# A fourth buffer for u, squares and gates left in PSUM, and another order for every engine

## The chip, the cores and the metric

The kernel runs on one core of a Trainium2 chip. The metric is device time in microseconds of one execution. The core has TensorE (PE), VectorE (DVE), ScalarE (ACT), GpSimd (POOL) and SyncE (SP), each with its own in-order list of instructions; DMA queues move data between device memory and the on-chip SBUF; matmul results land in PSUM, which has eight banks.

## The reference

Three layers follow one another, over 4 batches of 768 tokens with 384 channels.

```python
# attention: 8 heads of 48 channels, a state per head that decays by channel
f = 1.0 / (1.0 + np.exp(-f_logit))
for t in range(S):
    state = f[:, :, t, :, None] * state + np.einsum('bhd,bhe->bhde', k[:, :, t], v[:, :, t])
    y[:, :, t] = np.einsum('bhd,bhde->bhe', q[:, :, t], state)

# first MLP (x is y with the heads side by side)
h = gelu_tanh(x @ w_in)                       # 384 -> 1024
u, v = h[..., :512], h[..., 512:]
v_n = (v - mean(v)) / np.sqrt(var(v) + 1e-06) * g_ln
v_s = np.einsum('ts,bsd->btd', w_sg, v_n) + b_sg[None, :, None]
x = x + (u * v_s) @ w_out

# second MLP
h = np.maximum(x @ w_in2, 0.0)                # 384 -> 1024
conv = sum over 3 neighbouring tokens of conv_w[k] * h
out = (h * sigmoid(conv)) @ w_out2
```

## The kernel before, in words

**Units.** The attention is cut into 24 units, one per batch and chunk of 128 tokens (`Attention.plan`, L310). Four pairs of heads stand side by side on 112 partitions. One unit is a chain. SP loads the logits (`load_f`, L362), k and q (`load_kq`), and v. ScalarE takes the sigmoid (`decays`, L377). VectorE scans the decays forwards (`forth`, L383), takes the reciprocals of the ends (`turn`, L388), scans backwards (`back`, L396) and multiplies k and q by the products (`scale`, L408). TensorE transposes k (`turn_k`, L415: T in the text), ScalarE copies it (`keep_k`, L420), TensorE makes the state's update (`update`, L466: up). VectorE makes two states: the middle one (`middle`, L476, or a copy at L474 for a batch's first unit) and the one behind the unit (`behind`, L482 and L483), which the next unit needs. TensorE then multiplies q by the states (`states`, L496: st) and k by q (`scores`, L429: sc); VectorE masks the scores (`seen`, L436), and TensorE multiplies them by v (`values`, L512: va). ScalarE copies the output in two halves (`outs`, L525) and SP stores it.

**First MLP.** A batch's items stand in the string `SEQ`: L loads half of x (three units' outputs), v makes one 128-token part of v with its gelu and normalization (`vpart`: V), u one part of u with its gelu (`upart`: U), s one product with w_sg, which is scaled and gated (`sg`: S), and o one output (`out1`). Every fp32 operand is split into a high part (a ScalarE cast, L659) and a low part (a VectorE subtraction, L664), and each product is made of three matmuls (`mm3`, L653). The weights come as 64-bit numbers: one ScalarE pass (L578) and six VectorE instructions (`narrow_steps`, L579 to L591) narrow a piece.

**In a V**, ScalarE takes the gelu from the PSUM bank into SBUF with a sum (L908), GpSimd makes the mean (L911), ScalarE squares into a bf16 tile `junk` that nobody reads, for the sum alone (L914), GpSimd makes the root (L920, L921) and an offset (L924), ScalarE normalizes (L927). **In an S**, VectorE scales the bank into an SBUF tile `gt` (L996) and multiplies by u (L1002).

**What sets the order.** Every piece of work is a task, with the engine, an estimate of its time, the tasks that it follows, and the buffers that it takes and uses. `Order.run` goes through the tasks like a clock: of those of an engine that could begin soonest it writes the one with the lowest rank from the table `DUE`; then the engine's list is fixed. A task that takes a buffer of a ring (`RINGS`) waits there until the one that held it is free of its users. V, U and S take one of three PSUM banks (`M=3`); five more (`MA`) are opened when the attention is done. The second MLP follows (`second`).

Of the kernel before, what the change touches and what calls it, by code (L numbers as in the profile page):

```python
# [11 lines left out]
BF16 = mybir.dt.bfloat16  # L12
# [11 lines left out]
P = 128  # L24
# [43 lines left out]
class Order:  # L68
# [41 lines left out]
    def start(self, t):  # L110
        at = self.free[t.eng]
        for a in t.after:
            e = a.end + (HOP if a.eng != t.eng or a.kb else 0.0)
            if e > at:
                at = e
        for n in t.take:
            e, _ = self.soonest(n)
            if e is None:
                return None
            if e > at:  # L120
                at = e
# [32 lines left out]
    def write(self, at, t):  # L154
# [32 lines left out]
        -548.7, -477.3, -161.3, -153.1, 189.4, 212.0, 364.9, 430.2, 591.1, 816.0, 698.7, 736.9,  # L187
        909.1, 1157.3, 1295.0, 1375.7, 1376.1, 1739.4, 1653.8, 1761.4, 3751.4, 2011.8, 2225.9, 3838.8,
    ],
    "unit front": [  # L190
        1385.3, 859.0, 1060.5, -250.2, 1511.2, 1703.3, 1812.9, 2025.9, 2365.2, 229.0, 604.9, 1897.4,
        3788.3, 1201.6, 3779.5, 3805.2, 631.9, 182.0, 1139.5, 3820.9, 1390.5, 1533.0, 2401.4, 499.2,
    ],
    "unit": [
        638.3, 737.0, -203.3, 127.0, 277.0, 425.3, 534.2, 705.8, 1362.3, -576.0, 881.6, 507.0,
        -609.2, -479.0, 1608.3, 211.3, -646.7, -160.9, 210.1, 700.3, 716.4, 533.3, 2213.5, 868.7,
    ],
    "unit out": [
        2412.2, 992.5, 1073.9, 2426.6, 757.2, -615.8, 2198.6, -642.0, 890.0, 1138.3, 1022.7, 1151.8,
        197.2, 624.4, 886.7, 466.3, 991.0, 1980.1, 2189.4, 1392.3, 2317.7, 1151.9, 471.3, 1300.2,  # L200
    ],
    "weight load": [
# [3 lines left out]
    ],  # L206
    "weight": [
# [21 lines left out]
    ],  # L229
    "item then": [  # L230
# [20 lines left out]
POOL_RATE = 0.0021  # L251

# [9 lines left out]
class Attention:  # L262
# [12 lines left out]
    def __init__(self, nc, tc, ctx, cst, f, kq, v, xd):  # L275
# [21 lines left out]
        self.stored, self.scaled = {}, []  # L297

# [7 lines left out]
    def plan(self, S, u):  # L306
# [9 lines left out]
        lf = add("SP", 0.38, self.load_f, kind="unit load", take=["ft"], kb=224)  # L316
        lk = add("SP", 0.38, self.load_kq, kind="unit load", take=["kin"], kb=448)
        lv = add("SP", 0.38, self.load_v, kind="unit load", take=["vt"], kb=192)
        ft, kin, vt = lf.hold["ft"], lk.hold["kin"], lv.hold["vt"]
        sig = add("ACT", 0.63, self.decays, lf, kind="unit front", uses=[ft], table="sigmoid")  # L320
        fw = add("DVE", 1.23, self.forth, sig, kind="unit front", uses=[ft], take=["pr"])
# [4 lines left out]
        kq = add("DVE", 1.23, self.scale, bw, lk, kind="unit front", uses=[pr, kin])  # L326
        self.scaled.append(kq)
        tr = add("PE", 0.6, self.turn_k, kq, uses=[kin], take=["T"])
        k2 = add("ACT", 0.53, self.keep_k, tr, uses=[tr.hold["T"]], take=["k2"])
        up = add("PE", 0.8, self.update, k2, lv, self.scored, uses=[k2.hold["k2"], vt], take=["A"])  # L330
        a1 = up.hold["A"]
        mid = add("DVE", 0.36, self.middle, up, before, uses=[a1], take=["mid"])
# [11 lines left out]
        s7 = self.scored = add("PE", 0.92, self.scores, s5, kq, uses=[kin], take=["A"])  # L344
# [7 lines left out]
        s6 = add("PE", 0.78, self.values, cm, s5, lv, uses=[a2, cm.hold["sm"], vt])  # L352
# [117 lines left out]
    def middle(self, u, st):  # L470

        mid = st["mid"] = self.wp.tile([R, NP, D], F32, tag="mid", bufs=2, name="mid")
        if u % NCH == 0:
            self.nc.vector.tensor_copy(mid, st["pu"][0:R, 0])  # L474
        else:
            self.nc.vector.tensor_tensor(mid, st["pu"][0:R, 0], self.st[u - 1]["new"], op=ALU.add)  # L476

    def behind(self, u, st):
# [4 lines left out]
        self.nc.vector.tensor_tensor(new, new, pe, op=ALU.mult)  # L483
# [122 lines left out]
class Mlp:  # L606


    RINGS = dict(M=3, early=2, stg=2, x0=1, x1=1, vg=2, u=3, xr=2, gt=1)
# [85 lines left out]
    def low(self, n, terms, lo, after, rank, uses):  # L695
# [10 lines left out]
        m = box["m"] = S.add("PE", 0.25 + n * 0.0023, mm, after=after, rank=rank, take=["bank"], uses=uses)  # L706
# [61 lines left out]
    def prep(self, w_in, w_sgt, w_out, g_ln, conv_w, b_sg, pace):  # L768
# [5 lines left out]
        self.junk = self.mp.tile([P, FH], BF16, name="junk")  # L774
# [45 lines left out]
        t3, hold, c = self.narrow(conv_w.bitcast(I32).rearrange("p (n two) -> p n two", two=2), "early", 12, [pace[2]])  # L820
        t3 = S.add("DVE", 0.17, lambda: nc.vector.tensor_copy(self.cols[:, KH:], c()), after=[t3], rank=due("weight", 12), uses=[hold])
        self.t_w["g"] = [t, t2, t3]
# [20 lines left out]
    def load_x(self, b, hf, after, item):  # L843
# [11 lines left out]
        ld = S.add("SP", 0.38, load, after=after, rank=due("item", item), take=["stg"], kb=590)  # L855
# [34 lines left out]
    def vpart(self, b, n, item):  # L890
# [38 lines left out]
        m = box["m"] = S.add("PE", 2.09, mm, after=self.t_x[b, hf] + self.t_w["v"], rank=rank, take=["bank", "vg"], uses=[x])  # L929
# [4 lines left out]
        t = S.add("ACT", 0.93, square, after=[t], rank=then, uses=[vg])  # L934
# [15 lines left out]
    def upart(self, b, hf, db, item):  # L950
# [12 lines left out]
        def gelu():  # L963
            u = self.u[b, hf, db] = self.mp.tile([P, HALF], F32, tag="u", bufs=3, name="u")
# [4 lines left out]
            1.57,  # L969
# [558 lines left out]
```

## Time and profile before

| | us |
|---|---|
| median of 3 runs | 598.56 (597.53 to 599.43) |
| the profiled execution, its own time | 596.89 |
| its span in the trace | 595.2 |
| TensorE busy | 547.0 (92% of the span) |
| VectorE busy | 440.7 (74%) |
| ScalarE busy | 361.8 (61%) |
| GpSimd busy | 68.1 (11%) |
| mean granted TensorE clock | 0.988 |

The profiled execution is 1.67 us under the median of the runs. Its span leaves out 1.7 us around it. In tables of stretches, the busy time of each engine stands beside the number of its instructions; in a timeline, the bracket at a row's end is the idle time just before it and what ended it.

### The profile page before, as it was taken

The page shows a single profiled execution, that of the slowest core. Times are in us where ns is not written, and L with a number is a line of the kernel's source. Part 1 is how long each engine was busy: PE and PEld are TensorE (multiplying, and loading weights), DVE is VectorE, ACT ScalarE, POOL GpSimd, SP SyncE. Part 2 cuts the span into 40 slices and gives each one's busy share as a digit, 9 for nine tenths or more (in the row PEclk, how much of TensorE's full clock was granted, in tenths as well). Part 3 has the DMA queues.
Part 4 walks back from the last instruction along what each step waited for, and adds up shares of the span by engine and source line. Part 5 has one row for each costly group of instructions (what it writes and reads, how often), then busy time and mean ns, then how long its engine had stood idle before and what let it go on. Part 6 is the DMA issues. An engine that isn't in the chain of part 4 may idle for free.

```text
span 595.2 us, 13752 instructions
## 1 busy us (share of the span) xinstructions
PE 547.0 (92%) x5561; PEld 513.9 (86%) x5561; DVE 440.7 (74%) x775; ACT 361.8 (61%) x720; POOL 68.1 (11%) x152
## 2 busy tenths in 40 slices
PE   2553887999999999999999999999999999999995
PEld 2442676998888889889999999999999999999995
DVE  6999998999986986986855444788687685866730
ACT  2534789456788264785347722788777585775830
POOL 2000142000422000433004210110000000000000
PEclk9999987999999999999999999999999999999998
DMA  8777466236858645376334450640210202110011
GB/s 256 198 201 209 133 195 176 78 110 170 205 137 208 182 143 156 99 164 129 95 109 97 131 102 1 152 52 11 81 54 28 67 13 81 39 43 28 14 41 44
DMA packets 63367, 65.89 MB, mean 111 GB/s; under 512 B 26560, under 2 KB 55872, under 8 KB 63296
## 3 DMA queue, kind: packets, MB, share of 16 engines
q1 hardware_dynamic: 59840, 60.22, 35.2%
q0 software_dynamic: 3456, 4.72, 5.8%
q8 instruction: 45, 0.74, 0.5%
q14 instruction: 26, 0.21, 0.1%
HBM read 47.62 MB, written 17.30 MB: 109 GB/s over the span
## 4 chain that ended last, share of the span: by engine, by line
PE 74%; DVE 14%; ACT 4%; DMA 3%; POOL 2%; issue 2%; ACTq 0%; DVEq 0%; POOLq 0%
PE mm L653 36%; PE ma L653 31%; DVE kin L408 2%; DVE pr L396 2%; DVE pr L383 2%; PE at L496 1%; PE at L429 1%; PE at L466 1%; PE at L512 1%; DMA ft<-in_f_pairs 1%; PE pk L415 1%; POOL mv L921 1%; DMA stg<-in_moe_w_out 1%; DVE sm L436 1%; ACT junk L914 1%
## 5 line engine op out<-in xcount | busy, mean ns | idle before, releaser
L1173 DVE SCALAR_TENSOR_TENSOR cv<-h,cols,cv 128x384 f32<-128x384 f32 x128 | 76.1, 615 | 20.7 <-ACT cv L1177 20.2
L653 PE MATMUL mm<-wsg,vn 128*128 128x384 f32 x432 | 81.3, 342 | 0.0
L653 PEld LDWEIGHTS mm<-wsg,vn 128*128 128x128 f32 x432 | 75.8, 190 | 0.9
L653 PE MATMUL ma<-xx,win 128*128 128x386 f32 x378 | 70.3, 338 | 0.0
L653 PEld LDWEIGHTS ma<-xx,win 128*128 128x128 f32 x378 | 66.7, 188 | 0.0
L653 PE MATMUL ma<-wout,gh 128*128 128x384 f32 x224 | 57.4, 337 | 0.0
L653 PE MATMUL mm<-x,win 128*128 128x384 f32 x234 | 48.0, 352 | 1.5 <-ACT win L659 1.0
L653 PE MATMUL mm<-win,x 128*128 128x512 f32 x180 | 47.7, 413 | 0.0
L664 DVE TENSOR_TENSOR gl<-cv,gh 128x384 fp32r<-128x384 f32 x64 | 35.5, 555 | 16.2 <-ACT gh L659 15.5
L1183 DVE TENSOR_TENSOR cv<-cv,h 128x384 f32<-128x384 f32 x64 | 35.4, 554 | 13.0 <-ACT cv L1180 12.9
L653 PEld LDWEIGHTS mm<-x,win 128*128 128x128 f32 x234 | 41.1, 192 | 3.1 <-ACT win L659 1.4
L1177 ACT ACTIVATE cv<-h,cols 128x384 f32<-128x384 f32 x64 | 39.5, 616 | 3.9 <-DVE gl L664 2.0
L653 PE MATMUL mm<-wout,gh 128*128 128x384 f32 x160 | 41.0, 337 | 0.0
L653 PEld LDWEIGHTS ma<-wout,gh 128*128 128x128 f32 x224 | 40.6, 187 | 0.0
L653 PEld LDWEIGHTS mm<-win,x 128*128 128x128 f32 x180 | 34.0, 196 | 7.5
L415 PE MATMUL pk<-ident,kin 112*128 112x112 f32 (+1 forms) x96 | 16.3, 300 | 25.5 <-DVE kin L408 25.3
L653 PE MATMUL mm<-xx,win 128*128 128x386 f32 x198 | 38.2, 338 | 0.0
L653 PE MATMUL ma<-wout,gl 128*128 128x384 f32 x112 | 37.7, 337 | 0.0
L653 PE MATMUL mm<-g,wout 128*128 128x384 f32 x192 | 36.6, 340 | 0.0
L659 ACT CAST gh<-cv 128x384 fp32r<-128x384 f32 x64 | 32.4, 506 | 6.2 <-DVE cv L1183 6.1
L415 PEld LDWEIGHTS pk<-ident,kin 112*128 112x128 f32 (+1 forms) x96 | 11.4, 154 | 27.8 <-issue 11.5
L653 PEld LDWEIGHTS mm<-xx,win 128*128 128x128 f32 x198 | 35.1, 188 | 0.0
(122 smaller groups left out, 1129.1 us busy)
## 6 DMA issues: line engine op xcount, KB each, us to landing
kin<-in_kq_pairs SPq DMA_DIRECT2D x24, 448.0 KB, 4.6
stg<-xd SPq DMA_DIRECT2D x16, 576.0 KB, 4.2
ft<-in_f_pairs SPq DMA_DIRECT2D x24, 224.0 KB, 3.6
vt<-in_v_tokens SPq DMA_DIRECT2D x24, 192.0 KB, 3.8
xd<-o SPq DMA_DIRECT2D x96, 48.0 KB, 2.7
stg<-in_moe_w_out SPq DMA_DIRECT2D x12, 384.0 KB, 4.2
xd<-xr POOLq DMA_DIRECT2D x24, 192.0 KB, 4.6
out<-oo SPq DMA_DIRECT2D x24, 192.0 KB, 1.9
```

What stands on the lines that cost most here:

```text
L383: self.nc.vector.tensor_tensor_scan(st["pr"][:, 1], st["f"][:, 0:n], self.first, 1.0, op0=ALU.mult, op1=ALU.max)
L396: self.nc.vector.tensor_tensor_scan(backward(st["pr"][:, 0]), backward(st["f"][:, 1 : n + 1]), backward(self.last), 1.0, op0=ALU.mult, op1 ...
L408: self.nc.vector.tensor_tensor(st["kq"], st["kq"], pr, op=ALU.mult)
L415: self.nc.tensor.transpose(pk[:nk, j, 0:R], st["kq"][:, 0, j, 0:nk], self.cst["ident"][0:R, 0:R])
L429: self.nc.tensor.matmul(sc[ts, a, j, :], kt[sl, j, ts], qt[sl, j, ts], start=True, stop=True)
L436: self.nc.vector.copy_predicated(sm, mask, st["sc"])
L653: self.nc.tensor.matmul(out, l[a], r[b], start=i == 0 and m == 0, stop=i == n - 1 and m == 2)
L659: "ACT", 0.2 + n * 0.0008, lambda: nc.scalar.copy(hi(), src()), after=[after, *wait], rank=rank, uses=uses
L664: lambda: nc.vector.tensor_tensor(lo(), src(), hi(), op=ALU.subtract),
L1173: nc.vector.scalar_tensor_tensor(c, h, self.conv(w, fb), c, op0=ALU.mult, op1=ALU.add)
L1177: nc.scalar.activation(box["c"], box["h"][:, 1 : HALF + 1], AF.Copy, scale=self.conv(1, fb))
L1183: nc.vector.tensor_tensor(box["c"], box["c"], box["h"][:, 1 : HALF + 1], op=ALU.mult)
```

## The change

Five things change in the code, and with them the order of nearly everything.

1. u has four buffers instead of three. `junk` and `gt` are gone: the square writes back into its PSUM bank, which is held until the square is done, and the scaling of an S writes back into its bank, from which the gate reads; the bank is held until the gate is done.
2. The host pads the logits to 517 columns a row, -200 at the start of each pair of heads and at the end. The load is one run of 2068 B per row instead of four of 512 B, the sigmoid runs over all 517 columns, and the six memsets that zeroed the gaps are gone.
3. The first middle state of each batch (units 0, 6, 12, 18) is copied by ScalarE instead of VectorE. (A set for the state behind is empty.)
4. The narrowing of conv_w moves from the ring `early` to the ring `stg` and follows a later unit; only the second MLP's first tap waits for it.
5. The table `DUE` has new numbers, a task on another engine than TensorE counts 0.3 us from TensorE's end, some estimates change, and chains named `was` keep units and items of one kind in their order.

```diff
@@ DUE (all tables, one line shown)
-        1385.3, 859.0, 1060.5, -250.2, 1511.2, 1703.3, 1812.9, 2025.9, 2365.2, 229.0, 604.9, 1897.4,
+        771.9, 6249.9, 6239.8, 304.5, -121.0, 475.0, 760.8, 488.3, 655.8, 538.5, 6880.0, 542.2,
...
+FIRST_ON_ACT = {0, 6, 12, 18}
+STATE_ON_ACT = set()
@@ Order.start
-            e = a.end + (HOP if a.eng != t.eng or a.kb else 0.0)
+            e = a.end + (0.0 if a.eng == t.eng and not a.kb else HOP_PE if a.eng == "PE" else HOP)
@@ Attention.__init__
-        for t in self.fts:
-            nc.gpsimd.memset(self.pairs(t)[:, :, 0:1], 0.0)
-            nc.gpsimd.memset(t[:, n : n + 1], 0.0)
@@ Attention.plan
-        lf = add("SP", 0.38, self.load_f, kind="unit load", take=["ft"], kb=224)
+        was = self.was
+        lf = add("SP", 0.38, self.load_f, was.get("f"), kind="unit load", take=["ft"], kb=224)
...
-            mid = add("DVE", 0.36, self.middle, up, before, uses=[a1], take=["mid"])
+        if n == 0 and u in FIRST_ON_ACT:
+            mid = add("ACT", 0.36, self.middle, up, uses=[a1], take=["mid"])
+        else:
+            mid = add("DVE", 0.36, self.middle, up, before, uses=[a1], take=["mid"])
@@ Attention.load_f, decays
-        self.nc.sync.dma_start(self.pairs(st["f"])[:, :, 1:W1], self.f[divmod(u, NCH)])
+        self.nc.sync.dma_start(st["f"], self.f[divmod(u, NCH)])
...
-        f = self.pairs(st["f"])[:, :, 1:W1]
-        self.nc.scalar.activation(f, f, AF.Sigmoid)
+        self.nc.scalar.activation(st["f"], st["f"], AF.Sigmoid)
@@ Mlp
-    RINGS = dict(M=3, early=2, stg=2, x0=1, x1=1, vg=2, u=3, xr=2, gt=1)
+    RINGS = dict(M=3, early=2, stg=2, x0=1, x1=1, vg=2, u=4, xr=2)
@@ Mlp.prep
-        t3, hold, c = self.narrow(conv_w.bitcast(I32).rearrange("p (n two) -> p n two", two=2), "early", 12, [pace[2]])
+        t3, hold, c = self.narrow(conv_w.bitcast(I32).rearrange("p (n two) -> p n two", two=2), "stg", 12, [pace[7]])
@@ vpart
-                self.junk, box["v"], AF.Square, bias=box["s"][:, 1:2], accum_out=box["s"][:, 2:3]
+                box["p"], box["v"], AF.Square, bias=box["s"][:, 1:2], accum_out=box["s"][:, 2:3]
...
-        t = S.add("ACT", 0.93, square, after=[t], rank=then, uses=[vg])
+        t = S.add("ACT", 0.93, square, after=[t], rank=then, uses=[m.hold["bank"], vg])
@@ sg
-            box["t"] = self.mp.tile([P, HALF], F32, tag="gt", name="gt")
             nc.vector.scalar_tensor_tensor(
-                box["t"], box["p"], self.cols[:, db : db + 1], self.bb[:, ts], op0=ALU.mult, op1=ALU.add
+                box["p"], box["p"], self.cols[:, db : db + 1], self.bb[:, ts], op0=ALU.mult, op1=ALU.add
...
-            nc.vector.tensor_tensor(u, box["t"], u, op=ALU.mult)
+            nc.vector.tensor_tensor(u, box["p"], u, op=ALU.mult)
...
-        t = S.add("DVE", 0.62, scale, after=[m] + self.t_w["g"], rank=then, take=["gt"], uses=[m.hold["bank"]])
-        t = S.add("DVE", 0.56, gate, after=[t, tu], rank=then, uses=[hu, t.hold["gt"]])
+        t = S.add("DVE", 0.62, scale, after=[m] + self.t_w["g"], rank=then, uses=[m.hold["bank"]])
+        t = S.add("DVE", 0.56, gate, after=[t, tu], rank=then, uses=[hu, m.hold["bank"]])
```

What the new numbers do is seen in the lists of instructions. Two places matter below; lines of the kernel after are some 11 to 20 higher than those of before.

VectorE before, around S0, the first product with w_sg: `vn` is the normalized v of a batch, `wsg` w_sg, and S0 reads the low part of `vn` that the sixth row makes.

```order
L482 TENSOR_TENSOR new<-at,mid 112x192
L483 TENSOR_TENSOR new<-new,pend 112x192
L664 TENSOR_TENSOR vn_138<-vg,vn_137 128x512
L664 TENSOR_TENSOR wsg_130<-early,wsg_130 128x768
L436 COPY_PREDICATED sm_100<-seen,at 128x512
L664 TENSOR_TENSOR vn_138<-vg,vn_137 128x512
L664 TENSOR_TENSOR wout<-stg,wout 128x384
L383 SCALAR_TENSOR_TENSOR pr<-ft_88,first 112x516
```

The row that S0 waits for stands behind the last low part of w_sg, and the scans of the next unit follow.

VectorE after, around S0: it needs the low part of `wsg` in the seventh row, and the `mm` rows are its own scaling and gate.

```order
L601 TENSOR_SCALAR stg<-stg 128x384
L602 SCALAR_TENSOR_TENSOR stg<-stg 128x384
L610 SCALAR_TENSOR_TENSOR stg<-stg 128x384
L490 TENSOR_TENSOR mid<-at,new 112x192
L683 TENSOR_TENSOR wsg_123<-early,wsg_123 128x768
L683 TENSOR_TENSOR wout<-stg,wout 128x384
L683 TENSOR_TENSOR wsg_124<-early,wsg_124 128x768
L448 COPY_PREDICATED sm_95<-seen,at 128x512
L1016 SCALAR_TENSOR_TENSOR mm<-mm,cols,bb 128x384
L1022 TENSOR_TENSOR u<-mm,u 128x384
```

S0's last operand now is a part of w_sg, ahead of which a piece of w_out (`stg`) is narrowed; 178 instructions stand up to it, where 150 stood up to the row before.

TensorE before, around S0: states and scores of unit 8, its values, then S0.

```order
L496 MATMUL at<-kin,new 48x64 x2
L496 MATMUL at<-kin,mid 48x64 x2
L429 MATMUL at<-kin 64x64 x16
L512 MATMUL at<-sm_100,vt 48x64 x16
L653 MATMUL mm<-wsg_130,vn_137 128x384 x2
L653 MATMUL mm<-wsg_130,vn_138 128x384
L653 MATMUL mm<-wsg_130,vn_137 128x384 x2
L653 MATMUL mm<-wsg_130,vn_138 128x384
```

S0 follows the values of unit 8 and the V parts of the first batch, ahead of unit 9.

TensorE after, around S0: the last of the states of unit 11, its scores, then S0, whose fifth row is the first to read the late part of `wsg`.

```order
L515 MATMUL at<-kin,new 48x64 x2
L515 MATMUL at<-kin,mid 48x64 x2
L515 MATMUL at<-kin,new 48x64 x2
L515 MATMUL at<-kin,mid 48x64 x2
L515 MATMUL at<-kin,new 48x64 x2
L515 MATMUL at<-kin,mid 48x64 x2
L441 MATMUL at<-kin 64x64 x16
L672 MATMUL mm<-wsg_123,vn_132 128x384 x2
L672 MATMUL mm<-wsg_123,vn_133 128x384
L672 MATMUL mm<-wsg_123,vn_132 128x384 x2
L672 MATMUL mm<-wsg_123,vn_133 128x384
L672 MATMUL mm<-wsg_124,vn_132 128x384 x2
```

S0 now stands behind the scores of unit 11 instead of the values of unit 8.

## Rows read from the trace of the kernel before

**Rows 1.** Stretches: length, busy PE, PEld, DVE, ACT, POOL (instructions), granted clock, DMA share, GB/s

```profile
75.00:100.00 25.00, 18.69 (x357) 15.51 (x355) 22.44 (x37) 21.06 (x44) 10.06 (x17) 0.86 0.68 196
100.00:110.00 10.00, 9.92 (x78) 9.74 (x79) 8.49 (x13) 6.42 (x13) 0.00 (x0) 0.83 0.53 153
101.10:125.00 23.90, 23.81 (x276) 22.43 (x273) 21.00 (x38) 12.90 (x23) 0.00 (x0) 0.95 0.28 74
125.00:588.70 463.70, 463.03 (x4070) 442.01 (x4068) 330.23 (x587) 290.86 (x581) 51.65 (x104) 1.00 0.37 95
```

**Rows 2.** Timeline of TensorE: start us, us, engine, line, operation, tiles, count

```profile
63.85 2.34 PE L653 MATMUL mm<-win,x 128*128 128x512 f32 x9
...
66.12 0.26 PE L496 MATMUL at<-kin,new 48*48 48x64 f32 x2
...
101.11 7.61 PE L653 MATMUL mm<-wsg,vn 128*128 128x384 f32 x36
...
112.23 0.68 PE L466 MATMUL at<-vt,k 64*64 64x48 f32 x32
...
112.83 1.86 PE L653 MATMUL mm<-x,win 128*128 128x384 f32 x9
...
114.62 0.26 PE L496 MATMUL at<-kin,new 48*48 48x64 f32 x2
...
116.21 3.42 PE L653 MATMUL mm<-wsg,vn 128*128 128x384 f32 x18
...
588.35 0.33 PE L653 MATMUL mm<-wout,gl 128*128 128x384 f32 x1
```

**Rows 3.** Timeline of VectorE, columns as before

```profile
5.28 1.23 DVE L383 TENSOR_TENSOR_SCAN pr<-ft,first 112x516 f32<-112x516 f32 x1 [5.28 <-ACT ft L377]
...
47.48 0.35 DVE L476 TENSOR_TENSOR mid<-at,new 112x192 f32<-112x192 f32 x1
...
48.26 0.36 DVE L483 TENSOR_TENSOR new<-new,pend 112x192 f32<-112x192 f32 x1
48.54 0.68 DVE L664 TENSOR_TENSOR win<-early,win 128x512 fp32r<-128x512 f32 x1
...
64.25 0.35 DVE L579 TENSOR_SCALAR stg<-stg 128x384 f32<-128x384 f32 x1
...
67.10 0.17 DVE L579 TENSOR_SCALAR early<-early 128x24 f32<-128x24 f32 x1
...
75.06 1.22 DVE L383 TENSOR_TENSOR_SCAN pr<-ft,first 112x516 f32<-112x516 f32 x1
...
78.95 0.68 DVE L664 TENSOR_TENSOR vn<-vg,vn 128x512 fp32r<-128x512 f32 x1
...
100.21 0.69 DVE L664 TENSOR_TENSOR vn<-vg,vn 128x512 fp32r<-128x512 f32 x1 [0.18 <-ACT vn L659]
```

**Rows 4.** VectorE by line, 0 to 110: busy, mean ns | idle before, releaser

```profile
L436 DVE COPY_PREDICATED sm<-seen,at 128x512 f32<-128x512 int32 x9 | 6.5, 725 | 0.7 <-PE at L429 0.5
...
L664 DVE TENSOR_TENSOR vn<-vg,vn 128x512 fp32r<-128x512 f32 x6 | 4.1, 688 | 0.9 <-ACT vn L659 0.9
...
L664 DVE TENSOR_TENSOR x<-stg,x 128x384 fp32r<-128x384 f32 x6 | 3.0, 550 | 1.3 <-ACT x L659 1.3
...
L664 DVE TENSOR_TENSOR x<-stg,x 128x1152 fp32r<-128x1152 f32 x6 | 8.1, 1350 | 1.5 <-ACT x L659 1.5
```

**Rows 5.** Whole span by line: TensorE, ScalarE, GpSimd, VectorE; columns as before

```profile
L653 PE MATMUL mm<-x,win 128*128 128x384 f32 x234 | 48.0, 352 | 1.5 <-ACT win L659 1.0 <-DVE win L664 0.2 <-ACT u L965 0.2
...
L914 ACT ACTIVATE junk<-vg,mv 128x512 bf16<-128x512 f32 x24 | 17.4, 723 | 3.9 <-POOL mv L911 3.7
...
L914 ACT ACTIVATION_READ_ACCUMULATOR junk<-vg,mv 128x1 f32 x24 | 4.5, 189 | 0.0
...
L911 POOL TENSOR_SCALAR mv<-mv 128x1 f32<-128x1 f32 x24 | 8.8, 366 | 179.9 <-ACT vg L908 179.7
...
L1002 DVE TENSOR_TENSOR u<-gt,u 128x384 f32<-128x384 f32 x32 | 17.8, 555 | 10.2 <-ACT u L965 9.6
```

More of the change, by code (lines that the diff above doesn't have):

```diff
@@ L297, in __init__ @@
         self.stored, self.scaled = {}, []
+        self.was = {}
     @staticmethod
@@ L314, in add @@
             return S.add(eng, us, lambda: fn(u, st), after=after, rank=due(kind, u), **kw)
-        lf = add("SP", 0.38, self.load_f, kind="unit load", take=["ft"], kb=224)
-        lk = add("SP", 0.38, self.load_kq, kind="unit load", take=["kin"], kb=448)
-        lv = add("SP", 0.38, self.load_v, kind="unit load", take=["vt"], kb=192)
+        was = self.was
+        lf = add("SP", 0.38, self.load_f, was.get("f"), kind="unit load", take=["ft"], kb=224)
+        lk = add("SP", 0.38, self.load_kq, was.get("k"), kind="unit load", take=["kin"], kb=448)
+        lv = add("SP", 0.38, self.load_v, was.get("v"), kind="unit load", take=["vt"], kb=192)
         ft, kin, vt = lf.hold["ft"], lk.hold["kin"], lv.hold["vt"]
         sig = add("ACT", 0.63, self.decays, lf, kind="unit front", uses=[ft], table="sigmoid")
-        fw = add("DVE", 1.23, self.forth, sig, kind="unit front", uses=[ft], take=["pr"])
+        fw = add("DVE", 1.23, self.forth, sig, was.get("s"), kind="unit front", uses=[ft], take=["pr"])
         pr = fw.hold["pr"]
@@ L326, in plan @@
         kq = add("DVE", 1.23, self.scale, bw, lk, kind="unit front", uses=[pr, kin])
+        was.update(f=lf, k=lk, v=lv, s=kq)
         self.scaled.append(kq)
-        tr = add("PE", 0.6, self.turn_k, kq, uses=[kin], take=["T"])
-        k2 = add("ACT", 0.53, self.keep_k, tr, uses=[tr.hold["T"]], take=["k2"])
-        up = add("PE", 0.8, self.update, k2, lv, self.scored, uses=[k2.hold["k2"], vt], take=["A"])
+        tr = add("PE", 0.45, self.turn_k, kq, was.get("t"), uses=[kin], take=["T"])
+        k2 = add("ACT", 0.53, self.keep_k, tr, was.get("c"), uses=[tr.hold["T"]], take=["k2"])
+        up = add("PE", 0.7, self.update, k2, lv, self.scored, uses=[k2.hold["k2"], vt], take=["A"])
         a1 = up.hold["A"]
-        mid = add("DVE", 0.36, self.middle, up, before, uses=[a1], take=["mid"])
+        if n == 0 and u in FIRST_ON_ACT:
+            mid = add("ACT", 0.36, self.middle, up, uses=[a1], take=["mid"])
+        else:
+            mid = add("DVE", 0.36, self.middle, up, before, uses=[a1], take=["mid"])
         md = mid.hold["mid"]
@@ L337, in plan @@
         if more:
-            new = self.news[u] = add("DVE", 0.72, self.behind, mid, pe, uses=[a1, md], take=["new"])
-        s5 = add("PE", 0.95, self.states, mid, kq, before, uses=[kin, md], take=["A"])
+            if u in STATE_ON_ACT:
+                own = add("DVE", 0.36, self.behind, mid, uses=[a1, md], take=["new"])
+                new = self.news[u] = add("ACT", 1.3, self.decayed, own, pe, uses=[own.hold["new"]])
+                new.hold = own.hold
+            else:
+                new = self.news[u] = add("DVE", 0.72, self.behind, mid, pe, uses=[a1, md], take=["new"])
+        s5 = add("PE", 0.64, self.states, mid, kq, before, uses=[kin, md], take=["A"])
         a2 = s5.hold["A"]
@@ L343, in plan @@
             before.hold["new"].left += 1
-        s7 = self.scored = add("PE", 0.92, self.scores, s5, kq, uses=[kin], take=["A"])
+        s7 = self.scored = add("PE", 0.7, self.scores, s5, kq, uses=[kin], take=["A"])
         a3 = s7.hold["A"]
@@ L351, in plan @@
             cm = add("DVE", 0.72, self.seen, s7, uses=[a3], take=["sm"])
-        s6 = add("PE", 0.78, self.values, cm, s5, lv, uses=[a2, cm.hold["sm"], vt])
+        s6 = add("PE", 0.7, self.values, cm, s5, lv, was.get("o"), uses=[a2, cm.hold["sm"], vt])
+        was.update(t=tr, c=k2, o=s6)
         self.stored[u] = []
@@ L472, in middle @@
         mid = st["mid"] = self.wp.tile([R, NP, D], F32, tag="mid", bufs=2, name="mid")
-        if u % NCH == 0:
+        if u in FIRST_ON_ACT:
+            self.nc.scalar.copy(mid, st["pu"][0:R, 0])
+        elif u % NCH == 0:
             self.nc.vector.tensor_copy(mid, st["pu"][0:R, 0])
@@ L482, in behind, with decayed @@
         self.nc.vector.tensor_tensor(new, st["pu"][0:R, 1], st["mid"], op=ALU.add)
-        self.nc.vector.tensor_tensor(new, new, pe, op=ALU.mult)
+        if u not in STATE_ON_ACT:
+            self.nc.vector.tensor_tensor(new, new, pe, op=ALU.mult)
+    def decayed(self, u, st):
+        for j in range(NP):
+            self.nc.scalar.activation(st["new"][:, j], st["new"][:, j], AF.Copy, scale=self.pend[0:R, u, j : j + 1])
     def states(self, u, st):
@@ L704, in mm @@
                 nc.tensor.matmul(box["p"], self.cst[name], x, start=i == 0, stop=i == len(t) - 1)
-        m = box["m"] = S.add("PE", 0.25 + n * 0.0023, mm, after=after, rank=rank, take=["bank"], uses=uses)
+        m = box["m"] = S.add("PE", 0.25 + n * 0.0025, mm, after=after, rank=rank, take=["bank"], uses=uses)
         return S.add(
@@ L853, in tiles @@
             self.x[b, hf] = [self.mp.tile([P, KC, HALF], F32R, tag=f"x{hf}{i}", name=f"x{hf}{i}") for i in range(2)]
-        ld = S.add("SP", 0.38, load, after=after, rank=due("item", item), take=["stg"], kb=590)
+        ld = S.add("SP", 0.38, load, after=[*after, self.was.get("x")], rank=due("item", item), take=["stg"], kb=590)
+        self.was["x"] = ld
         new = S.add("ACT", 0.0, tiles, after=[ld], rank=rank, take=[f"x{hf}"])
@@ L927, in norm @@
             nc.scalar.activation(box["v"], box["v"], AF.Identity, bias=box["s"][:, 1:2], scale=box["s"][:, 3:4])
-        m = box["m"] = S.add("PE", 2.09, mm, after=self.t_x[b, hf] + self.t_w["v"], rank=rank, take=["bank", "vg"], uses=[x])
+        m = box["m"] = S.add("PE", 2.12, mm, after=self.t_x[b, hf] + self.t_w["v"] + [self.was.get("v")], rank=rank, take=["bank", "vg"], uses=[x])
+        self.was["v"] = m
         self.all_in.append(m)
@@ L968, in upart @@
             "PE",
-            1.57,
+            1.62,
             mm,
-            after=self.t_x[b, hf] + self.t_w["u"],
+            after=self.t_x[b, hf] + self.t_w["u"] + [self.was.get("u")],
             rank=rank,
@@ L976, in upart @@
         self.all_in.append(m)
+        self.was["u"] = m
         t = S.add("ACT", 0.51, gelu, after=[m], rank=then, uses=[m.hold["bank"], m.hold["u"]], table="gelu")
@@ L1048, in first @@
     def first(self, stored):
+        self.was = {}
         for b in range(B):
@@ L1187, in in2_part @@
         t = S.add("ACT", 0.52, relu, after=[m, new], rank=k, uses=[m.hold["bank"]])
-        t = S.add("ACT", 0.62, tap1, after=[t], rank=k, take=["cv"])
+        t = S.add("ACT", 0.62, tap1, after=[t] + self.t_w["c"], rank=k, take=["cv"])
         cv = t.hold["cv"]
```

37 lines of the change are left out of this document (19 added, 18 removed), and 52 rows, old and new, of the table DUE.

## The prediction, on record before the run

> **What bounds the kernel now.** I read the stretches of the span first [rows 1]. From 125 us to the last matmul, which ends at 588.7, TensorE is idle for 0.7 of 463.7 us. In 75 to 100 us it is busy for 18.69 of 25. So the run is a head, in which TensorE waits, and a dense body, which is as long as the TensorE work left in it. The question is when the body begins, and how much work is left by then. TensorE's timeline [rows 2] gives the beginning: 101.11, with S0, the first product with w_sg; from there to 588.7 there are 487.6 us, and then 6.5 for the last copy and its store. VectorE's timeline [rows 3] gives what ends last before S0: its 150th instruction, the low part of a vn, runs from 100.21 to 100.90, and S0's first matmuls read it (the order above shows the place). VectorE starts at 5.28 and is at work nearly throughout. Laid end to end, with the start-to-start distances of these rows, its 150 pieces take 91.4 of the 95.6 us; the other 4.2 are waits, and the groups of its instructions [rows 4] name most of them: 1.3 for the x cast, 0.9 for the vn cast, 0.7 for scores.
>
> So the head is VectorE's, and the body TensorE's. A new order helps if VectorE has less to do ahead of S0, or if TensorE does more of its work in the head.
>
> **What moves.** No matmul is added or removed. Ahead of S0, TensorE now does for three more units T (turn_k), up (update), st (states) and sc (scores), two more va (values), two more V and one more U. In the dense stretch [rows 2] up takes 112.23 to 112.83, 0.60; U 112.83 to 114.62, 1.79; st, sc and T together 114.62 to 116.21, 1.59; va, as many matmuls as up, I take as 0.60; V 63.85 to 66.12, 2.27. That is 3 x 2.19 + 2 x 0.60 + 2 x 2.27 + 1.79 = **14.1 us** that the body no longer holds.
>
> On VectorE, S0 now waits for the last low part of w_sg as well. It is instruction 178 instead of 150. The 28 more are: three chains of scan, reciprocal, scan and product, 3.89 each (75.06 to 78.95 [rows 3]), 11.7; three middles and two pairs behind them, where a middle with its pair takes 1.06 (47.48 to 48.54), 2.5; one narrowing of six instructions, 2.85 (64.25 to 67.10); two masks, two low parts of w_out, one low part of a whole x [rows 4], 0.725, 0.550 (as for the half x, of the same shape) and 1.350, less the 0.08 by which a piece that reads nothing of its predecessor starts ahead of that one's end (48.26 and 0.36 against 48.54), 3.5; less the two first states that ScalarE now copies, 0.35 each as a middle, 0.7. The sum is 19.8. The new list puts unrelated pieces between the links of a chain more often; I take 0.7 off for that: **19.1 us**.
>
> VectorE's start stays: the narrowing piece that it now begins with needs one ScalarE pass, as the sigmoid was one, and the six small memsets on GpSimd that the first load waited for go. Without any wait the split would end at 5.3 + 91.4 + 19.1 = 115.8. I then went through the new lists piece by piece with these durations. The waits that I found come to 1.4 us (scores, the cast of the half x that is loaded behind unit 5's stores, the sigmoid behind a table load); the split ends at 117.2, and TensorE, which is then dense from V3 at about 90 on, itself reaches S0 at 117.6. With as many waits as before, 4.2, everything stands 2.8 later, 120.4. I take the middle, **119.0**, because each transfer in my walk had a quiet queue, and the head's queues are not quiet (DMA share 0.68 in 75 to 100 us [rows 1]).
>
> **Clock.** In 100 to 110 us TensorE was granted 0.83, after a stretch with gaps; in 101.1 to 125 the mean is 0.95, from 125 on 1.00 [rows 1]. Full speed is 2.4 GHz and the lower level 1.2, so S0 and S1 ran partly at 1.2. That cost 23.9 x 0.05 = 1.2 us of the body. In the new order TensorE has some 25 us of work in the 28 us ahead of S0, so the climb falls there, and the body saves **1.2**.
>
> **Sum.** S0 later by 119.0 - 101.1 = 17.9; less 14.1; less 1.2: +2.6. The profiled execution took 596.89; 599.5 is its new time. The median of the runs is 1.67 above that execution, so I forecast **601.2 us**. The ends of this case: 117.6 with the clock saved gives +1.2, 120.4 with nothing saved +5.2; 599.8 to 603.8. A difference under 0.3%, 1.8 us, counts as none.
>
> **What I cost at nothing.** The fourth buffer for u: TensorE waited for a u in one place, 0.2 us in all [rows 5]. The first states on ScalarE, four copies: ScalarE is busy for 21.06 of 75 to 100 us, but in my walk unit 6's copy, the only one in the dense part of the head, ends at 71.5, just as VectorE reaches the sum that reads it; if ScalarE is later there, VectorE waits behind the two squares ahead of the copy, up to 2 x 0.72 = 1.4 [rows 5], and some more for outputs. The logits in one run per row: the sigmoid gains five columns, and the loads are issued ahead. The narrowing of conv_w moves to another ring and is in both counts. The squares and gates in PSUM shorten or lengthen nothing in the sum; they hold banks, which is a rival.
>
> **Rivals.**
> *No change.* My walk is right about the waits: S0 at 117.6, and the climb costs what 100 to 110 us shows, 10 x 0.17 = 1.7. Then 16.5 - 14.1 - 1.7 = +0.7: 599.3. For it: TensorE's own work, not VectorE, then ends last ahead of S0, and it has little slack to lose. Against: it needs every load in time.
> *Faster.* VectorE never waits, and TensorE has no gap between V3 at 89.7 and S0: S0 at 115. Then 13.9 - 14.1 - 1.7, and the 0.7 us of gaps in the body goes too: -2.6, 596.0. Against: every load and every cast in the head would have to be early.
> *Slower, by banks.* Until the attention is done, V, U and S share three PSUM banks. A V's bank was free after its gelu; now it is held through GpSimd's mean and the square, 0.37 + 0.72 + 0.19 [rows 5], 1.3 us and the queue on ScalarE. An S's bank is held 0.555 longer, through the gate, and longer where VectorE takes a scan first. TensorE is in order: a piece that finds no free bank stops everything behind it. It decides where a bank is held for longer than the two pieces behind it take, 3.6 us for two U. If four of the sixteen V's behind S0 stall by 1.3 us, that is +5.2 on top: 606.4; for all gates, 32 x 0.555 more, 17.8: 619. Against: dense TensorE shows no bank wait before, and V is followed mostly by long pieces.
> The Trainium skill speaks against the change here: "ScalarE: Activation LUTs", section "Step-by-step: what each stage is for", calls PSUM the quicker destination for ScalarE, but only useful where TensorE does not need most of PSUM. No row here shows a square into PSUM; the sum would be the same by it.
> For VectorE reading a bank, this trace shows no price: a middle from a bank takes 0.35, as long as the product behind it in SBUF, 0.36 [rows 3]. "Perfetto Trace Analysis" of the Trainium skill, section "Optimizing Scalar/DVE Operations", gives some 125 ns of overhead for VectorE on PSUM against 60 on SBUF; by that, 64 scalings and gates would take an estimated 4.2 us more, and this rival would come that much nearer. The trace does not agree with it so far.
> *The change does not do what it says.* The fourth u buffer can be idle, since nothing waited for u; that is already in the sum, which rests on the order alone.
>
> **Chances.** The forecast 0.45, no change 0.25, faster 0.10, banks 0.20. Of the forecast's case a tenth lies within 1.8 us of before, as does a tenth of banks; a tenth of the no-change case lies beyond it. So faster 0.10, within 0.3% 0.29, slower 0.61. The range leaves out the faster case and the upper half of banks: 597.0 to 606.5.
>
> **What would show it.** The body's beginning: the first product with w_sg at 117.6 to 120.4, with the low part of w_sg or the scores just ahead of it, and 472 us, not 488, from there to the last matmul. The granted clock: 1.00 right behind S0, and the low stretch ahead of it. VectorE's waits until then: 1.4 to 4.2 us. If S0 comes at 119 and the body is longer than 474 us, TensorE's waits for a square or a gate must be there: banks. If S0 comes later than 121, my VectorE sum or a load is wrong; before 116, VectorE was not what bounded the head.

## The result and the profile after

The kernel after takes 605.86 us in the median of 4 runs (604.22 to 608.61), the kernel before beside it 598.33 (597.53 to 599.43): 1.0118 of its time, 95% interval 1.0084 to 1.0153. The change makes the kernel slower by 7.5 us. The forecast was 601.2; the range, 597.0 to 606.5, holds the time near its upper end. The forecast's own case ended at 603.8. The profiled execution took 604.22 us, the shortest of the four; its span is 602.2, 7.0 more than before.

The stretches of the kernel after, in the columns of [rows 1]:

```profile
50.00:75.00 25.00, 18.59 (x402) 14.92 (x402) 22.11 (x34) 14.51 (x31) 4.28 (x7) 0.72 0.75 200
75.00:100.00 25.00, 18.41 (x366) 15.30 (x367) 22.26 (x40) 17.89 (x34) 2.31 (x6) 0.67 0.67 180
...
100.00:110.00 10.00, 10.00 (x169) 8.75 (x168) 7.57 (x18) 7.69 (x18) 5.01 (x8) 1.00 0.68 195
125.05:595.70 470.65, 470.54 (x3970) 451.81 (x3965) 333.48 (x595) 293.19 (x584) 51.61 (x104) 1.00 0.34 89
```

The body has become shorter. The last matmul ends at 595.59, so the body is 470.54 us and has no gap (the 0.11 us that are not busy in the last row lie behind that matmul), against 487.6 with 0.8 of gaps [rows 1, 2]. The head has become longer by more: TensorE's timeline (columns as in [rows 2]) has S0 at 125.05 instead of 101.11.

```profile
60.39 1.10 PE L531 MATMUL at<-sm,vt 64*48 64x64 f32 x32 [0.85 <-DVE sm L448]
61.42 3.62 PE L672 MATMUL mm<-win,x 128*128 128x512 f32 x9
...
75.55 0.77 PE L515 MATMUL at<-kin,mid 48*48 48x64 f32 x10 [3.93 <-ACT mid L486]
...
94.67 1.11 PE L531 MATMUL at<-sm,vt 64*48 64x64 f32 x32 [1.02 <-DVE sm L448]
95.71 5.65 PE L672 MATMUL mm<-win,x 128*128 128x512 f32 x18
...
106.47 0.67 PE L531 MATMUL at<-sm,vt 64*48 64x64 f32 x32
...
125.05 6.53 PE L672 MATMUL mm<-wsg,vn 128*128 128x384 f32 x36
```

The account closes: S0 is 23.9 later and the body 17.05 shorter, which leaves 6.9 of the 7.0. What the rows of the head show:

- The values of a unit (`at<-sm,vt`, 32 matmuls) take 1.10 us at 60.39 and 94.67, where the granted clock, read in windows of 3 us, is 0.50, and 0.67 at 106.47, where it is 1.00. Between 65 and 74 it is 1.00 as well.
- TensorE waits 3.93 us for unit 6's first state on ScalarE.
- V3, the fourth V of the batch (the first nine of the 18 matmuls at 95.71), stands directly behind unit 8's values. From V3's start to S0 there are 29.3 us, of which TensorE waits 2.2.
- S0 follows the scores of unit 11 without a gap. The last low part of w_sg ends at 126.05, when S0 is already running, and S0 and S1 show no gap either. So TensorE's own list came last here, with VectorE close behind.

VectorE's waits up to the last low part of w_sg, grouped by what it waited for (engine, line <- releaser: us in total, times, longest):

```profile
DVE early L598 <- ACT early L597: 6.2, 1, 6.2
DVE sm L448 <- PE at L441: 2.8, 6, 0.8
DVE vn L683 <- ACT vn L678: 1.2, 2, 0.9
DVE mid L490 <- PE at L478: 1.1, 2, 1.0
DVE stg L598 <- ACT stg L597: 1.1, 1, 1.1
DVE wout L683 <- ACT wout L678: 1.0, 1, 1.0
DVE x L683 <- ACT x L678: 0.5, 1, 0.5
```

The first row is the start, 6.23 instead of 5.28 [rows 3]; the other six come to 7.7 us, against 3.2 before in the same view. Without start and waits VectorE's work up to 126.05 is 112.1 us, where the prediction had 110.5. The chain of what released what, from the T of unit 6 to the values ahead of V3 (start us, us, what), goes through GpSimd's statistics of the first two V and through the load of the second half of x:

```profile
68.97 0.55 PE pk L427 x4
...
69.59 0.53 ACT k L432
70.12 0.72 ACT mm L933 x2
...
71.19 2.19 POOL mv L940
...
75.82 0.83 ACT vg L946
...
76.67 0.63 ACT vn L678
...
77.32 0.69 DVE vn L683
...
82.33 0.93 DVE wsg L683
83.26 1.14 DVE kin L420
...
85.45 0.47 DVE wout L683
...
85.95 6.44 DMA stg<-xd
...
92.41 0.52 ACT x L678
...
92.95 1.03 DVE x L683 x2
93.98 0.65 DVE sm L448
...
94.67 1.11 PE at L531 x32
```

### The profile page after: what moved, and what is told of

Read it like the earlier page. It is cut to its first block, busy times and chain, and to the rows that moved or that the text cites. A ratio compares the mean times of both kernels' runs of the same rounds, so it can differ in the third digit from the quotient of the medians.

```text
span 602.2 us, 13717 instructions
## 1 busy us (share of the span) xinstructions
PE 547.6 (91%) x5561; PEld 514.4 (85%) x5561; DVE 441.1 (73%) x771; ACT 364.5 (61%) x724; POOL 71.5 (12%) x146
## 4 chain that ended last, share of the span: by engine, by line
PE 83%; DVE 10%; DMA 2%; ACT 2%; POOL 1%; issue 1%; DVEq 0%; ACTq 0%
PE mm L672 44%; PE ma L672 31%; PE at L515 2%; PE at L478 2%; PE at L531 2%; PE at L441 2%; DVE kin L420 2%; PE pk L427 1%; DVE pr L395 1%; DMA stg<-xd 1%; DVE pr L408 1%; DVE sm L448 1%; DMA early<-in_moe_w_in 1%; POOL mv L940 1%; DVE early L602 0%
## 5 line engine op out<-in xcount | busy, mean ns | idle before, releaser
L672 PEld LDWEIGHTS mm<-wsg,vn 128*128 128x128 f32 x450 | 78.1, 188 | 0.7
L672 PE MATMUL ma<-wout,gh 128*128 128x384 f32 x272 | 69.7, 337 | 0.0
L672 PE MATMUL ma<-xx,win 128*128 128x386 f32 x369 | 67.0, 338 | 0.0
L672 PE MATMUL mm<-win,x 128*128 128x512 f32 x198 | 54.3, 424 | 0.0
L672 PEld LDWEIGHTS ma<-wout,gh 128*128 128x128 f32 x272 | 49.4, 187 | 0.0
L672 PEld LDWEIGHTS mm<-win,x 128*128 128x128 f32 x198 | 38.9, 203 | 9.4 <-DVE x L683 0.4
L672 PE MATMUL mm<-x,win 128*128 128x384 f32 x234 | 46.0, 343 | 0.0
L672 PE MATMUL ma<-wout,gl 128*128 128x384 f32 x136 | 45.8, 337 | 0.0
L678 ACT CAST g<-u 128x384 fp32r<-128x384 f32 x32 | 16.4, 512 | 45.7 <-DVE u L1022 45.5
L1061 POOL DMA_DIRECT2D xd<-xr x24 | 21.4, 913 | 186.0 <-ACT xr L1058 143.0
```

The source lines that it names most:

```text
L672: self.nc.tensor.matmul(out, l[a], r[b], start=i == 0 and m == 0, stop=i == n - 1 and m == 2)
L678: "ACT", 0.2 + n * 0.0008, lambda: nc.scalar.copy(hi(), src()), after=[after, *wait], rank=rank, uses=uses
L1061: nc.gpsimd.dma_start(self.xd[b, hf][sl, :], box["x"], accum_op=ALU.add)
```

## Experiments

For these the order of every engine was written down as a list of tasks and replayed, so that a piece of code could change under one order, or one piece of an order move alone. Ratios are to the kernel before on the same chip.

**1. The code of the change, the order of before.** The added line says in words what the new loop does.

```diff
 def run(self):
-    at, t = min((c for c in can if c[0] <= soon), key=lambda c: (c[1].rank, c[0], c[1].n))
+    the task that stands first in the written list of the kernel before, and can begin
```

> All code edits of the change (u with four buffers, squares and gates in PSUM, first states on ScalarE, logits in one run, conv_w in the other ring), but every engine works through the list of the kernel before; only the narrowing of conv_w, which has another ring, comes some 45 VectorE instructions later, and one U late in the run swaps with its neighbour. Theory A (the order alone costs the time, because VectorE has 28 more pieces ahead of S0): 597 to 599, S0 at 99 to 101, no wait of TensorE for a square or a gate. Rival B (the banks held longer, or the first states behind ScalarE's queue, cost it): 601 to 606, with TensorE waits for a square, a gate or a middle state that the kernel before does not have.

602.24 us, ratio 1.0078 (1.0045 to 1.0111). S0 comes at 99.66, a little earlier than before, so theory A, the order alone, falls: the code costs time too, where the order is not made for it. Two more kernels take the code apart under this order.

**2. First states and one-run logits kept; squares, gates and u as before.**

> The list of the kernel before (conv_w's narrowing later), with the logits in one run and the first states on ScalarE, but the square in its SBUF tile, the scaling in its SBUF tile, and u with three buffers, as before. With squares and gates in PSUM the same list took 1.008 of the time before, with TensorE waits for u, x and a square of 6 us in 125 to 300. Theory B2 (the banks held longer cost this): 595.5 to 598.5, and those waits go. Rival: the first states or the one-run logits cost it: 600 to 603.

596.87, ratio 0.9996 (0.9974 to 1.0018). Under this order the first states and the logits cost nothing and bring nothing.

**3. Only the square back in SBUF; scaling and gate in PSUM, four buffers for u.**

```diff
-                box["p"], box["v"], AF.Square,
+                self.junk, box["v"], AF.Square,
-        t = S.add("ACT", 0.93, square, after=[t], rank=then, uses=[m.hold["bank"], vg])
+        t = S.add("ACT", 0.93, square, after=[t], rank=then, uses=[vg])
```

> The same list with only the scaling and gate left in PSUM (bank held until the gate) and four buffers for u; the square goes to its SBUF tile, so a V's bank is free after its gelu. If the square's hold is what costs: 596 to 598.5. If the gate's hold is: 600 to 603.

603.31, ratio 1.0080 (1.0058 to 1.0103), as with the square in PSUM. Putting the square back takes away TensorE's wait for a square (0.7 us in run 1) and no time. So under this order the cost comes with the gate in PSUM or with the fourth buffer for u, which runs 1 and 3 share and run 2 lacks; the two were not separated, and a square alone in PSUM was not run. The gate's longer hold is the likelier of the two, as a buffer more gives a task nothing to wait for. Where it goes is seen in one stretch, 125 to 300 us, of the three kernels (columns as in [rows 1]). With squares and gates in PSUM:

```profile
125.00:300.00 175.00, 169.22 (x2407) 150.22 (x2406) 142.02 (x251) 107.12 (x212) 33.53 (x60) 1.00 0.56 149
```

With the gates alone, and its longest wait:

```profile
125.00:300.00 175.00, 169.90 (x2397) 151.38 (x2397) 141.14 (x246) 107.03 (x212) 33.61 (x60) 0.98 0.57 149
...
PE mm L754 <- ACT u L1068: 3.4, 2, 2.7
```

The waiting products are S's, and what ends their wait is the gelu of a u. That the longer hold of a bank stands behind this wait is inferred from the runs, not read from the trace.

With neither:

```profile
125.00:300.00 175.00, 174.24 (x2439) 155.65 (x2438) 146.47 (x261) 108.39 (x214) 33.62 (x60) 1.00 0.58 154
```

TensorE loses 5.8, 5.1 and 0.8 us there. In the kernel after the same stretch is without a gap (the body above), so there the longer holds cost TensorE nothing. A run of the new order with both back in SBUF was not made.

**4. The new order, first states on VectorE.**

```diff
-FIRST_ON_ACT = {0, 6, 12, 18}
+FIRST_ON_ACT = set()
```

> The kernel after with its own order, but the four first states are copied by VectorE, at the place in the list where ScalarE had them. In the kernel after TensorE waits 3.9 us for unit 6's copy on ScalarE (behind two squares, two outputs and a normalization). Theory A (VectorE's list sets S0, this wait lies in its shadow): S0 at 124 to 126, time within 1 us of the kernel after, 604 to 607. Rival C (the late copy delays everything behind it): the 3.9 us wait goes and S0 comes 3 to 4 us earlier, 601 to 603.

605.70, ratio 1.0152 (1.0105 to 1.0199), S0 at 125.23. The wait did not go: TensorE now waits 4.5 us for the same state from VectorE. So who copies the state makes no difference, and rival C is not decided here; run 7 shortens the wait.

**5. The new order, two narrowings of w_out behind S0.** Tasks of two pieces moved in the written list; TensorE's list is unchanged.

> The kernel after, TensorE's list unchanged; two of the three narrowings of w_out that stand ahead of S0, with their high and low parts, come behind it (6.6 us of VectorE), and with the staging buffer free earlier the second half of x can be loaded earlier. Theory A: S0 some 6 us earlier, 118 to 120, the body 1 to 2 us longer because VectorE has that work there; 599 to 602. Rival D (waits for loads, casts and GpSimd's statistics set S0, not the length of VectorE's list): S0 at 123 to 125, 604 to 606.

607.26, ratio 1.0159 (1.012 to 1.0197). S0 at 126.35: VectorE has 6.6 us less to do ahead of it, and S0 is no earlier. Its waits in the head took the room (the three longest after the start):

```profile
DVE mid L567 <- PE at L555: 5.9, 4, 3.4
DVE sm L525 <- PE at L518: 4.9, 5, 2.5
DVE vn L760 <- ACT vn L755: 1.9, 2, 1.6
```

So VectorE's length, on which my sum was built, is by itself not what sets S0 in the new order. The test is not quite clean: two V's ahead of V3 take 4.2 us here and 3.6 in the kernel after, as TensorE ran slower there. The body, 473.05 us, is 2.5 longer; VectorE's moved work stands there.

**6. The order of before, one narrowing behind S0.**

> The kernel before, TensorE's list unchanged; the six narrowing instructions of one piece of w_out (2.85 us of VectorE) and one ScalarE pass come behind S0 instead of ahead of it. Theory A: S0 2 to 3 us earlier, 98 to 99, and 595.5 to 597 if the body hides the work. Rival D: S0 stays at 100 to 101, 598 to 599. If VectorE has no room in the body, S0 comes earlier and the time stays at 598.

599.07, ratio 1.0026 (1.0009 to 1.0044); S0 at 101.35. Here too 2.85 us less of VectorE's work did not bring S0 forward: the values ahead of S0 waited 2.6 us for the mask, 1.9 before. S0 and S1 take 8.35 us instead of 7.61, and the run is slower by 0.3%, with an interval that just leaves out no change.

**7. The new order, unit 6's state and unit 7's k ahead of the two normalizations on ScalarE**, and unit 8's k ahead of a sigmoid.

> The kernel after, with three pieces moved on ScalarE alone: unit 6's state copy and unit 7's k copy come ahead of the two normalizations that wait for GpSimd's roots (they stood behind or between them), and unit 8's k copy ahead of one sigmoid. Every other engine keeps its list. Theory E (ahead of S0 the units' chain runs through ScalarE's list, which waits for GpSimd's statistics of the first two V; VectorE's length is second): TensorE's 3.9 us wait for the state copy falls under 2, S0 3 to 5 us earlier, 120 to 122, time 600.5 to 603. Theory A (VectorE's list sets S0): S0 within 1 us of the kernel after, 604 to 606.

604.59, ratio 1.0118 (1.0075 to 1.0161), S0 at 124.18. The wait for the state fell from 3.9 to 1.9, and a wait of the scores for a VectorE state, 1.8, stands in its place. S0 is 0.9 earlier, and by the ratio nothing is gained: rival C of run 4, which wants 3 to 4 us, is not borne out.

**8. The moves of 5 and 7 together.**

> The same three pieces moved on ScalarE, and also two of the three narrowings of w_out behind S0, as in the run with the pieces late. Theory E with A behind it: with ScalarE's stalls shorter, the shorter VectorE list counts, S0 at 115 to 119 and 597 to 601. If the late pieces gain nothing here either, S0 as in the run before, and VectorE's length is no bound at all.

605.98, ratio 1.0133 (1.009 to 1.0177), S0 at 125.37. Theory E, that ScalarE's list and then VectorE's set S0, is not borne out either. Here too two V's take 4.2 us; the same moves with fillers (below) were not run.

**9. Fillers: transposes that nobody reads, in TensorE's gaps** (the helper alone is shown; it is called ahead of the update, the states and the values).

```diff
+    def fill(self, u, t, n):
+        if u in FILLED:
+            for _ in range(n):
+                self.nc.tensor.transpose(t[:, 1, 384:512], self.cst["ident"], self.cst["ident"])
```

In this run and the two that follow, the fillers ahead of the values open a new sum in the states' second bank, so that the states' part is lost there; all other instructions are as they were.

> The kernel after, with transposes that nobody reads put into TensorE's list ahead of the update (3), the states (3) and the values (4) of units 4 to 10, some 1.3 us of work per unit at full clock, mostly where TensorE waits; every other engine keeps its list. Theory F (between 50 and 95 us TensorE runs at the lower level, its granted clock is 0.50 to 0.87 in most stretches, the links of a unit's chain take 1.0 to 1.1 us instead of 0.6, and this delays everything behind): the granted clock of 50 to 100 us rises towards 1.00, the links take 0.6 to 0.7, S0 comes 2 to 5 us earlier, 120 to 123, time 600 to 604. Rival G (the links wait for other engines anyway, the clock lies in their shadow): S0 at 125 to 128, later by what the fillers cost, time 605 to 609.

603.24, ratio 1.0093 (1.0062 to 1.0124). The granted clock rises as expected, against 0.72 and 0.67:

```profile
50.00:75.00 25.00, 20.87 (x430) 17.01 (x432) 22.54 (x34) 14.90 (x32) 5.08 (x8) 1.00 0.75 209
75.00:100.00 25.00, 20.24 (x394) 16.31 (x395) 22.03 (x42) 18.33 (x33) 2.28 (x6) 0.86 0.66 175
```

The values of units 4 to 7 take 0.66 to 0.67, those of unit 8 still 1.11, and S0 is at 124.16, only 0.9 earlier. The interval overlaps that of the kernel after; this run by itself does not show a gain.

> The same fillers, and the three pieces moved on ScalarE. Theory F: 598 to 602, earlier than either alone. Rival G: 604 to 608.

601.35, ratio 1.0058 (1.0039 to 1.0076). This interval lies below that of the kernel after (1.0084 to 1.0153): clock and ScalarE's list together are worth some 3 to 4 of the 7 us. The profiled execution, the slowest of its six at 602.71, still has S0 at 124.27, so where the gain lies is not to be read from that trace.

**10. Fillers in the order of before**, in units 7 and 8.

> The list of the kernel before with one-run logits and first states on ScalarE, without squares and gates in PSUM (0.9996 of before), and fillers in units 7 and 8 alone: 4 ahead of the update, 4 ahead of the states, 6 ahead of the values. There the trace shows 1.82 us of work in 95 to 100, then S0 and S1 at 7.6 to 8.4 us instead of 6.3. Theory F: S0 and S1 take 6.3 to 7.0 us and the time falls by 1 to 2.5 us, 594.5 to 597 where before takes 597.7. Rival G: no difference, or 1 us slower.

596.87, ratio 0.9979 (0.9965 to 0.9994). The interval overlaps that of run 2, the same kernel without fillers, so no gain by the fillers is shown. S0 and S1 take 6.53 us, where 8.39 were taken without fillers (run 2):

```profile
98.84 6.53 PE L767 MATMUL mm<-wsg,vn 128*128 128x384 f32 x36
107.29 0.60 PE L512 MATMUL pk<-ident,kin 112*128 112x112 f32 x4 [1.93 <-DVE kin L505]
```

1.9 us come back, and 1.93 go into the next wait, for unit 9's k on VectorE. To keep the whole computation, the last run puts the fillers of the values into the scores' bank:

> The kernel before, every list as it was, with fillers in TensorE's list for units 7 and 8 alone: 4 ahead of the update, 4 ahead of the states, 6 ahead of the values, these last in the free columns of the scores' bank, so that the states' sum in their own bank is not opened anew. In the run with the old order filled, conv_w's narrowing stood ahead of unit 9 and held it up by 1.9 us behind S1; here it stands where it was. Theory F (the low clock at the head's end costs 1 to 2 us there): S0 and S1 take 6.5 us, unit 9's transposes wait less than 1 us, time 594.5 to 596.5 where before takes 598, ratio 0.994 to 0.998. Rival G: 598 to 599, the time goes into the wait for unit 9 or for the vn cast instead.

597.88, ratio 0.9999 (0.9985 to 1.0014): a miss. The fillers in the scores' bank, which VectorE still reads, wait 2.0 us for the mask and then stand 1.4 us between the mask and the values. S0 comes at 102.75 instead of 101.11, and S0 and S1 take 7.08 instead of 7.61. No version beat the kernel before and kept the whole computation.

**What the seven traces of the new order share.** The cast of the second half of x on ScalarE, V3, which reads it, and S0 begin at (us):

| kernel | cast | V3 | S0 |
|---|---|---|---|
| after | 92.41 | 95.71 | 125.05 |
| 4 | 92.74 | 96.04 | 125.23 |
| 5 | 94.57 | 97.98 | 126.35 |
| 7 | 91.16 | 94.47 | 124.18 |
| 8 | 93.49 | 96.79 | 125.37 |
| 9 | 91.62 | 94.99 | 124.16 |
| 9 with the moves of 7 | 90.72 | 94.02 | 124.27 |

In each, V3 follows the cast by 3.3 to 3.4 us, and S0 follows V3 by 28 to 30, of which TensorE waits 0.5 to 2.3. In each, two low parts of this half of x also stand on VectorE directly ahead of unit 8's mask, and so ahead of the values that V3 stands behind. In five of the seven ScalarE waits for the load of that half, which in the kernel after is issued at 85.95 and takes 6.44 us; the median of the 16 such loads is 4.2. No run moved this load, cast or mask, so that they set S0 is read from the traces and not tested.

## Why the prediction was right, and where it was off

- **Sign and shape** were right: the head grows by more than the body shrinks. The body was forecast at 472 us and is 470.5, and the granted clock is 1.00 behind S0. S0 and S1 take 6.53 instead of 7.61.
- **That the range held was luck.** 605.86 lies above the forecast's own case, 599.8 to 603.8. The range reached to 606.5 only for the lower half of the banks rival, and that rival did not happen in this kernel.
- **The size was off by 4.9 us** (7.5 measured, 2.6 forecast). The term is S0 at 119.0. It came at 125.05, 6.05 later, beyond the 120.4 that I gave as its upper end. The body, shorter by 17.05 instead of 15.3, gives 1.75 of that back; the other 0.6 lies behind the last matmul and between the profiled executions and the medians. By the prediction's own sign, S0 later than 121, the VectorE sum or a load is wrong.
- **The two steps that failed.** "The waits that I found come to 1.4 us", with 4.2 as the other end: VectorE's are 7.7, and 0.95 at the start, where its first piece is now a narrowing of weights; its work is also 1.6 longer than the sum. And "TensorE, which is then dense from V3 at about 90 on, itself reaches S0 at 117.6": V3 begins at 95.71, and from there to S0 TensorE takes 29.3 us instead of 27.6, with 2.2 of waits.
- **Why my walk found so few.** It used TensorE's pieces at their length in the dense stretch. In 50 to 100 us the values of three of the six units ran at 1.10 instead of 0.66, where the granted clock was 0.50. I had put the low clock ahead of S0 too, and booked that as a saving alone, covered by gaps; it lengthens the links of the units' chain there, and run 9 shows that the links shrink when the clock is up. Unit 6's copy, which the walk ends at 71.5, ends at 75.5, behind a normalization on ScalarE that waits for GpSimd. The prediction has no price for GpSimd's root; the first in the chain took 2.19 us. And the load of the second half of x, for which the walk had a quiet queue, took 6.44.
- **What I took for the bound was not it.** "The head is VectorE's" was read from 91.4 us of VectorE's pieces in 95.6. The chain view of the kernel before says otherwise: in the 42 us from 59 to S0, 6.0 us of the chain are VectorE's, 13.2 ScalarE's, 9.4 GpSimd's and 9.2 TensorE's. Its end (start us, us, what):

```profile
87.93 1.88 POOL mv L921
...
97.57 0.84 ACT wsg L659
...
98.43 0.96 DVE wsg L664
99.39 0.65 DVE sm L436
...
100.08 1.10 PE at L512 x32
101.18 7.54 PE mm L653 x36
```

  S0 stood directly behind unit 8's values there too. Runs 5, 6 and 8 take VectorE's work away, and S0 is no earlier. In the seven kernels of the new order it lies between 124.2 and 126.4, at most 0.9 us ahead of the kernel after. Units 6, 7 and 8 pass from TensorE to ScalarE to VectorE and back, with no U between; my reading is that several chains of nearly one length hold the head, and that the second half of x closes it, but that is argued. How much of the 7 us each holds stays open; only clock and ScalarE together have been shown to be worth something.
- **Banks.** The rival did not happen in the kernel after: no gap in the body. Under the order of before, where holds this long were not allowed for, the code cost 0.8%. The prediction had 5.2 us for four late squares and 17.8 for all gates; measured are 4.9 (run 1), the same with the gate and the fourth u alone (run 3) and nothing without them (run 2).
- **At nothing** I had put the first states, the logits and u. For the first states and the logits that is right by runs 2 and 4; u was not tested by itself.

## What to carry to other kernels

An engine that is busy for 93% of a stretch (VectorE, 89.2 of the 95.6 us ahead of S0 before) does not yet bound it: read the chain that ended last, move some of the engine's work out, and see whether the end follows. When a walk through a new order uses durations from a dense stretch, price the sparse one with durations that were measured in a sparse one. And a buffer that is held longer is tested under the order that was made for the shorter hold as well as under its own: the two say different things.

## What was not expected of the hardware

- A square into its PSUM bank takes 0.690 us, into SBUF 0.723 [rows 5]; the SBUF tile was bf16 and the bank is fp32, so place and type change together. That agrees with the Trainium skill, "ScalarE: Activation LUTs", section "Step-by-step: what each stage is for".
- VectorE's scaling takes 0.623 into PSUM and took 0.615 into SBUF, reading its bank both times; the gate takes 0.556 with one operand from PSUM and 0.555 from SBUF alone [rows 5]. The price for PSUM that the Trainium skill gives in "Perfetto Trace Analysis", section "Optimizing Scalar/DVE Operations", is not seen in these two; the measurement decides. The scaling before, then scaling, gate and square after:

```profile
L996 DVE SCALAR_TENSOR_TENSOR gt<-mm,cols,bb 128x384 f32<-128x384 f32 x24 | 14.8, 615 | 11.4 <-PE mm L653 11.2
...
L1016 DVE SCALAR_TENSOR_TENSOR mm<-mm,cols,bb 128x384 f32<-128x384 f32 x25 | 15.6, 623 | 14.7 <-PE mm L672 14.7
L1022 DVE TENSOR_TENSOR u<-mm,u 128x384 f32<-128x384 f32 x25 | 13.9, 556 | 0.7
...
L933 ACT ACTIVATE mm<-vg,mv 128x512 f32<-128x512 f32 x22 | 15.2, 690 | 5.3 <-POOL mv L930 5.2
```

- Ten transposes per unit were enough to speed TensorE up in the middle of the head. In the kernel after, the values of unit 4 take 1.10 us and the V behind them 3.62; with the fillers (first two rows) they take 0.67 and 2.34. The granted clock of a stretch has to be read beside such durations: in run 5, without fillers, the row of 50 to 75 us reads 1.00 as in the filled kernel, and yet the same two pieces (last two rows) take 1.11 and 4.21.

```profile
60.81 0.67 PE L621 MATMUL at<-sm,vt 64*48 64x64 f32 x32 [0.27 <-DVE sm L528]
61.41 2.34 PE L762 MATMUL mm<-win,x 128*128 128x512 f32 x9
...
50.00:75.00 25.00, 20.07 (x402) 15.88 (x402) 20.70 (x31) 12.79 (x28) 2.85 (x5) 1.00 0.62 175
...
60.76 1.11 PE L608 MATMUL at<-sm,vt 64*48 64x64 f32 x32 [0.85 <-DVE sm L525]
61.80 4.21 PE L749 MATMUL mm<-win,x 128*128 128x512 f32 x9
```
